# Products queued behind the attention work, four weight-sum tiles, and the first block's attention placed anew

## The chip, the cores and the metric

The kernel runs on one core of a Trainium2 chip. The metric is the device time of one execution in microseconds (us). TensorE (PE) does the matrix products, VectorE (DVE), ScalarE (ACT) and GpSimd (POOL) the elementwise work, and SyncE (SP) issues the transfers. Each engine works through its own instructions in the order in which the program has them.

## The reference

```python
# q, k, v: (8, 8, 576, 64); chunks of 64 tokens, each attends to itself alone
scores = scale * np.matmul(q_c, k_c.transpose(0, 1, 2, 4, 3))
scores = scores - np.max(scores, axis=-1, keepdims=True)
attn = np.exp(scores)
attn = attn / (np.sum(attn, axis=-1, keepdims=True) + 1e-09)
out = np.matmul(attn, v_c)
x = out.transpose(0, 2, 1, 3).reshape(4608, 512)
# layer 1: gated MLP, d_ff 1536
g = x @ w_gate
x = (g * (1.0 / (1.0 + np.exp(-g))) * (x @ w_val)) @ w_out
# layer 2: RMS norm times rms_g, and a gated MLP with weights of its own
xn = x / np.sqrt(np.mean(x * x, axis=-1, keepdims=True) + 1e-06) * rms_g
g = xn @ w_gate2
return (g * (1.0 / (1.0 + np.exp(-g))) * (xn @ w_val2)) @ w_out2
```

## The kernel before

Every matrix product is done as three products of a high part and a low part of its operands (`mm3`). Layer 1 takes the 4608 tokens in nine blocks of 512 and walks for each block through twelve steps f, each of 128 of the 1536 hidden columns (the loop from L1000 on). A step is: `emit_g` (12 matmuls into the bank "g", the sigmoid on ScalarE, the gate product on VectorE), run(0), `emit_v` (12 matmuls into the bank "v", the value product on VectorE, its high part `hh` cast on ScalarE), run(1), `emit_y` of the step before (12 matmuls that add into four output banks), then `lo()`, which is VectorE's low part `hl`, and run(2). The banks "g" and "v" have one buffer each: the matmuls of the next gate can't begin until VectorE has read the gate of this step.

What the three runs of a step do stands in a table `at`: a block has 36 positions, three a step, so position 24 is run(0) of step 8. The table places beside layer 1 of a block

- the attention of the next block, four tiles of 128 tokens, beginning at b = 0, 8, 16 and 24: transposes of queries and keys (`trans_att`, or `trans_tok` for the first tiles), scores and exponential (`att_s`), the division (`att_n`), transposes of the probabilities (`att_td` in two halves of eight small transposes on VectorE, for tiles from 8 on; `att_t` through TensorE before), the product with the values (`att_pv`) and the split of x (`att_lo`, whose tiles are `xh` and `xl`);
- the RMS norm of the block before, with a Newton iteration on VectorE and GpSimd at position 26 (L538 to L547) and the scaling at 28 to 34 (L555);
- in blocks 1 to 6 the weights of layer 2, of which sums and differences are formed: each of seven a group is copied by ScalarE (L175), its rest subtracted by GpSimd, and the pair written to memory by SP. These pairs stand in tiles "ws" of which there are two.

Loads of queries, keys and values for a later group are spread over positions by `spread`. In the first block (`head`) each run also holds a conversion of layer-1 weights, `conv1`: ScalarE's rebase and cast, four VectorE instructions (L115, L118, L121, L139) and a low part that SP writes to memory; and the loop issues what is left of the first groups' loads, the list `later`, 16 a step. Layer 2 follows in another loop (from L750 on) that the change does not reach.

Of the kernel before, what the change touches and what calls it, by code (L numbers as in the profile page):

```python
# [9 lines left out]
F32 = mybir.dt.float32  # L10
F32R = mybir.dt.float32r
# [8 lines left out]
def tile_kernel(  # L20
# [17 lines left out]
    nc = tc.nc  # L38
# [3 lines left out]
    P = 128  # L42
# [24 lines left out]
    cv = open_pool(conv, "cv", 3, "right")  # L67
# [84 lines left out]
    HK = KD * P // 2  # L152
# [18 lines left out]

    def comb_split(nm, fp, k):
        t = comb[nm, fp][k]
        w = cv.tile([P, 2, HK], F32R, tag="ws", bufs=2, name=f"ws{nm}{fp}_{k}")
        nc.scalar.copy(w[:, 0], t)  # L175
        nc.gpsimd.tensor_sub(w[:, 1], t, w[:, 0].bitcast(F32))
        nc.sync.dma_start(out=w2_d["gvo".index(nm), fp, :, k], in_=w.bitcast(F32))
# [14 lines left out]
    EARLY = NW // P + 1  # L192
# [20 lines left out]
    def load_qk(g):  # L213
        tq = ax.tile([P, HP, 10, 32], F32, tag="xq", name=f"xq_{g}")
        tk = ax.tile([P, HP, 10, 32], F32, tag="xk", name=f"xk_{g}")
        gt[g] = [tq, tk]
        dmas = []
        for hp in range(HP):
            for t, src in ((tq, q), (tk, k)):
                for o, m, b, s in segs_of(g):  # L220
                    for z in range(4):
                        hpar, e = divmod(z, 2)
                        dmas.append((
                            t[32 * z:32 * z + 32, hp, 2 * o:2 * (o + m), :],
                            src[b, 2 * hp + hpar, s:s + m * CH, 32 * e:32 * e + 32].rearrange(
                                "(tb p) i -> p tb i", p=32
                            ),
                        ))
        return dmas

    def load_v(g):
        if g == 0:
            tv = xp.tile([P, HP, len(groups[g]), D], F32, tag="xl", name="xv_0")
        else:
            tv = ax.tile([P, HP, 5, D], F32, tag="xv", name=f"xv_{g}")
        gt.setdefault(g, [None, None]).append(tv)
        dmas = []
        for o, m, b, s in segs_of(g):
            for n in range(m):
                for hpar in range(2):  # L240
                    z = hpar ^ ((groups[g][0] + o + n) % 2)
                    dmas.append((
                        tv[64 * z:64 * z + 64, :, o + n, :],
                        v[b, hpar::2, s + n * CH:s + (n + 1) * CH, :].rearrange("h p d -> p h d"),
                    ))
        return dmas
# [39 lines left out]
    def issue(dmas):  # L286
        for o, i in dmas:
            nc.sync.dma_start(out=o, in_=i)  # L288
# [145 lines left out]
    def emit_g(l, j, f):  # L434
        n = blocks[j][1]
        xh, xl = xhl[l, j]
        wh, wl = w_of(l, j, f, "g")
        g = ps.tile([P, 512], F32, tag="g", name=f"g{l}_{j}_{f}")
        for c in range(KD):
            mm3(g[:, :n], wh[:, c], wl[:, c], xh[:, c, :n], xl[:, c, :n], c == 0, c == KD - 1)  # L440
        sg = hp_.tile([P, 512], F32, tag="sg", name=f"sg{l}_{j}_{f}")
        nc.scalar.activation(sg[:, :n], g[:, :n], AF.Sigmoid)  # L442
        nc.vector.tensor_mul(sg[:, :n], g[:, :n], sg[:, :n])  # L443
        return sg

    def emit_v(l, j, f, sg):
        n = blocks[j][1]
        xh, xl = xhl[l, j]
        wh, wl = w_of(l, j, f, "v")
        vv = ps.tile([P, 512], F32, tag="v", name=f"v{l}_{j}_{f}")  # L450
        for c in range(KD):
            mm3(vv[:, :n], wh[:, c], wl[:, c], xh[:, c, :n], xl[:, c, :n], c == 0, c == KD - 1)
        nc.vector.tensor_mul(sg[:, :n], vv[:, :n], sg[:, :n])  # L453
        hh = hp_.tile([P, 512], F32R, tag="hh", name=f"hh{l}_{j}_{f}")
        hl = hp_.tile([P, 512], F32R, tag="hl", name=f"hl{l}_{j}_{f}")
        nc.scalar.copy(hh[:, :n], sg[:, :n])  # L456
        hid[l, j, f] = (hh, hl)
        return lambda: nc.vector.tensor_sub(hl[:, :n], sg[:, :n], hh[:, :n].bitcast(F32))  # L458

    def emit_y(l, j, f):  # L460
        n = blocks[j][1]
# [111 lines left out]
    def spread(l, j, pos, n, make):  # L573
        todo = []

        def step(z):
            if z == 0:
                todo.extend(make())
            issue(todo[z * len(todo) // n:(z + 1) * len(todo) // n])

        for z in range(n):
            put(l, j, pos + z, lambda z=z: step(z))

    for x, (l, j) in enumerate(seq):
        if x + 1 < len(seq):
            nl, nj = seq[x + 1]
            if nl == 0:
                for n, i in enumerate(tiles_of(nj)):
                    b = 8 * n
                    if i >= EARLY:  # L590
                        put(l, j, b - 1, lambda i=i: trans_att(i))
                    else:
                        put(l, j, b, lambda i=i: trans_tok(i, ("a0", "a1")))
                    e = 1 if i < 8 else 0
                    put(l, j, b + 1 + e, lambda i=i: att_s(i))
                    put(l, j, b + 2 + e, lambda i=i: att_n(i))
                    if i < 8:
                        put(l, j, b + 6, lambda i=i: att_t(i))
                    else:
                        put(l, j, b + 3, lambda i=i: att_td(i, 0))  # L600
                        put(l, j, b + 4, lambda i=i: att_td(i, 1))
                    e = 0 if i < 8 else 1
                    put(l, j, b + 8 - e, lambda i=i, nj=nj: att_pv(i, nj))
                    put(l, j, b + 9 - e, lambda i=i, nj=nj: att_lo(i, nj))
                    for c in (2 * i, 2 * i + 1):
                        g = where[c][0]
                        if g > 0 and c == groups[g][-1] and g + 2 < len(groups):
                            spread(l, j, b + 1, 8, lambda g=g: load_qk(g + 2))
                            spread(l, j, b + 9, 3, lambda g=g: load_v(g + 2))
        if x > 0 and seq[x - 1][0] == 0:  # L610
            pj = seq[x - 1][1]
            for d in range(KD):
                put(l, j, 3 + 2 * d, lambda pj=pj, d=d: rms_sq(pj, d))
            put(l, j, 12, lambda pj=pj: rms_split(pj))
            put(l, j, 14, lambda pj=pj: rms_mm(pj))
            for z in range(4):
                put(l, j, 18 + 2 * z, lambda pj=pj, z=z: rms_rec(pj, z))
            put(l, j, 26, lambda pj=pj: rms_newton(pj))
            for d in range(KD):
                put(l, j, 28 + 2 * d, lambda pj=pj, d=d: rms_x(pj, d))  # L620
# [3 lines left out]
    for (nm, f), (j, pos) in zip(w2, slots):  # L624
# [3 lines left out]
        if f >= NP2:  # L628
            fp = f - NP2
# [279 lines left out]
    with tc.manual_schedule():  # L909
# [48 lines left out]
        later = load_v(1) + load_qk(2) + load_v(2)  # L958
# [35 lines left out]
        lp = 0  # L994
# [5 lines left out]
        for n, (l, j, f) in enumerate(iters):  # L1000
            def run(p):
                for fn in at.get(3 * n + p, ()):
                    fn()

            head = (l, j) == (0, 0)
            if (j, f) == (1, 0):
                conv.close()
                cv = open_pool(conv, "cv2", 2, "right")
            if (j, f) == (NB - 1, 0):
                conv.close()  # L1010
                attn.close()
                X2 = open_pool(two, "x2", 1, "right")
                x_load(0, 0)
                xops = x_prep(0, 0)
            if (j, f) == (NB - 1, 8):
                x_load(0, 1)
                xops = xops + x_prep(0, 1)
            if (j, f) == (NB - 1, 8):
                load_ring(16)

            if head:
                issue(later[lp:lp + 16])
                lp += 16
            if n + 2 < len(iters) and n + 2 >= NF:
                load_lo(*iters[n + 2])
            sg = emit_g(l, j, f)
            run(0)
            if head:
                conv1(3 * f + 7)
            lo = emit_v(l, j, f, sg)  # L1030
            run(1)
            if head:
                conv1(3 * f + 8)
            if prev is not None:
                emit_y(*prev)
                if prev[2] == NF - 1:
                    evac_y(*prev[:2])
            lo()
            run(2)
            if head:  # L1040
                conv1(3 * f + 9)
            if j == NB - 1 and f >= 2:
                for _ in range(3 if f > 6 else 2):
                    if xops:
                        xops.pop(0)()
            prev = (l, j, f)
# [108 lines left out]
```

## Time and profile before

| what | value |
|---|---|
| median of 3 runs | 1873.76 us (1873.12 to 1874.0) |
| the profiled execution's own time | 1874.61 us |
| its span in the profile | 1872.8 us |
| mean granted TensorE clock | 0.983 |
| PE busy | 1787.9 us, 95% of the span |
| DVE busy | 1262.1 us, 67% |
| ACT busy | 743.5 us, 40% |
| POOL busy | 385.6 us, 21% |
| moved by DMA | 379.60 MB, mean 203 GB/s |

The busy shares are means over stages that differ much, and the span is what the profiler saw between the first and the last instruction; the execution's own time lies 1.8 us above it. A granted clock of 1 is 2.4 GHz, and 0.5 is 1.2 GHz. In a row of a timeline the brackets hold the engine's idle time just before the instruction and what ended it.

### The profile page before, as it was taken

How to read it: one execution, taken by the hardware profiler on the slowest of the kernel's cores; microseconds unless marked ns; L12 is line 12 of the kernel's file. 1: busy time of each engine (PE TensorE's matmuls, PEld its weight loads, DVE VectorE, ACT ScalarE, POOL GpSimd, SP SyncE). 2: the span in 40 equal slices, each digit the busy share in tenths (PEclk: the TensorE clock that was granted, in tenths of full speed). 3: DMA queues.
4: the chain of work that ended last, by engine and by line, in shares of the span. 5: the costliest groups of instructions: out<-in, count | busy, mean ns of one | idle time of the engine just before them, and what ended most of it. 6: DMA issues, size and time to landing. Idle time of an engine off the chain costs nothing.

```text
span 1872.8 us, 31073 instructions
## 1 busy us (share of the span) xinstructions
PE 1787.9 (95%) x11070; PEld 1520.7 (81%) x11070; DVE 1262.1 (67%) x2366; ACT 743.5 (40%) x1312; POOL 385.6 (21%) x391
## 2 busy tenths in 40 slices
PE   6688999999999999999999999999999999999999
PEld 4466877777787777777888878998898889999999
DVE  7787686776777777776654465864594568468465
ACT  4454343433344342443323233533353345235334
POOL 1000333234342342534011310110020011002000
PEclk7899999999999999999999999999999999999999
DMA  9785657767577766566343567677667767887875
GB/s 245 164 254 161 170 179 218 212 172 213 162 216 196 224 200 207 174 194 208 107 138 94 192 172 250 196 242 208 200 210 227 209 188 221 264 264 252 279 246 180
DMA packets 389546, 379.60 MB, mean 203 GB/s; under 512 B 204560, under 2 KB 240400, under 8 KB 389392
## 3 DMA queue, kind: packets, MB, share of 16 engines
q1 hardware_dynamic: 389392, 377.61, 67.7%
q8 instruction: 89, 1.46, 0.3%
q14 instruction: 65, 0.53, 0.1%
HBM read 316.15 MB, written 61.34 MB: 202 GB/s over the span
## 4 chain that ended last, share of the span: by engine, by line
PE 64%; DVE 13%; DMA 7%; ACT 6%; SPq 4%; issue 3%; POOL 3%; ACTq 0%; DVEq 0%; POOLq 0%
PE ygA L862 5%; PE yvA L862 4%; PE g L430 3%; DVE pT L364 3%; PE g L432 3%; PE g L431 3%; PE v L430 3%; PE v L432 2%; PE v L431 2%; PE ygC L862 2%; PE y L430 2%; PE y L432 2%; PE y L431 2%; SPq L288 2%; PE yvC L862 2%
## 5 line engine op out<-in xcount | busy, mean ns | idle before, releaser
L430 PE MATMUL g<-xh,wg 128*128 128x512 f32 x432 | 176.7, 409 | 27.6 <-DVE sg L443 26.5
L456 ACT CAST hh<-sg 128x512 fp32r<-128x512 f32 x108 | 67.0, 621 | 273.7 <-DVE sg L453 273.7
L431 PE MATMUL g<-xl,wg 128*128 128x512 f32 x432 | 172.5, 399 | 1.6 <-DVE xl L424 1.6
L443 DVE TENSOR_TENSOR sg<-g,sg 128x512 f32<-128x512 f32 x108 | 74.0, 685 | 147.2 <-ACT sg L442 147.0
L432 PE MATMUL g<-xh,lg 128*128 128x512 f32 x432 | 172.0, 398 | 0.7 <-DMA lg<-lo_scratch 0.7
L430 PE MATMUL v<-xh,wv 128*128 128x512 f32 x432 | 171.2, 396 | 1.3 <-DVE sg L453 1.3
L430 PE MATMUL y<-hh,wo 128*128 128x512 f32 x432 | 172.2, 399 | 0.0
L431 PE MATMUL y<-hl,wo 128*128 128x512 f32 x432 | 169.6, 393 | 2.0 <-DVE hl L458 1.9
L431 PE MATMUL v<-xl,wv 128*128 128x512 f32 x432 | 169.0, 391 | 0.0
L432 PE MATMUL v<-xh,lv 128*128 128x512 f32 x432 | 168.9, 391 | 0.0
L432 PE MATMUL y<-hh,lo 128*128 128x512 f32 x432 | 168.7, 390 | 0.0
L802 POOL TENSOR_TENSOR h<-h,h 128x512 f32<-128x512 f32 (+1 forms) x30 | 37.1, 1236 | 551.4 <-DVE h L780 551.4
L364 DVE STREAM_TRANSPOSE pT<-p 32x128 f32<-32x128 f32 x448 | 135.4, 302 | 12.8 <-POOL p L348 6.6
L838 DVE TENSOR_TENSOR hl<-h,hh 128x512 fp32r<-128x512 f32 (+1 forms) x180 | 121.4, 699 | 13.7 <-ACT hh L837 13.6
L430 PEld LDWEIGHTS g<-xh,wg 128*128 128x128 f32 x432 | 83.0, 192 | 54.1 <-DVE sg L443 35.4
L837 ACT CAST hh<-h 128x512 fp32r<-128x512 f32 (+1 forms) x180 | 99.0, 576 | 41.9 <-PE yvA L862 26.6
L763 ACT ACTIVATE sig<-sgt 128x512 f32<-128x512 f32 (+1 forms) x90 | 53.0, 589 | 156.8 <-DVE sgt L771 156.8
L442 ACT ACTIVATE sg<-g 128x512 f32<-128x512 f32 x108 | 64.5, 598 | 93.9 <-PE g L432 93.2
L453 DVE TENSOR_TENSOR sg<-v,sg 128x512 f32<-128x512 f32 x108 | 73.4, 680 | 40.4 <-PE v L432 37.8
L348 POOL TENSOR_TENSOR p<-p,r 128x512 f32<-128x512 f32 x36 | 39.5, 1098 | 292.2 <-DVE r L347 242.7
L764 DVE TENSOR_TENSOR sgt<-sgt,sig 128x512 f32<-128x512 f32 (+1 forms) x90 | 57.7, 641 | 61.6 <-ACT sig L763 61.6
L432 PEld LDWEIGHTS g<-xh,lg 128*128 128x128 f32 x432 | 83.4, 193 | 19.4 <-DMA lg<-lo_scratch 1.1
(770 smaller groups left out, 4686.3 us busy)
## 6 DMA issues: line engine op xcount, KB each, us to landing
wrg<-w_scratch SPq DMA_DIRECT2D x210, 256.0 KB, 3.1
wrv<-w_scratch SPq DMA_DIRECT2D x210, 256.0 KB, 3.1
wro<-w_scratch SPq DMA_DIRECT2D x210, 256.0 KB, 3.0
lg<-lo_scratch SPq DMA_DIRECT2D x96, 256.0 KB, 2.9
lv<-lo_scratch SPq DMA_DIRECT2D x96, 256.0 KB, 3.2
lo<-lo_scratch SPq DMA_DIRECT2D x96, 256.0 KB, 4.0
w_scratch<-wsg SPq DMA_DIRECT2D x42, 256.0 KB, 2.1
w_scratch<-wsv SPq DMA_DIRECT2D x42, 256.0 KB, 2.5
```

Source lines behind the costliest of these rows:

```text
L364: nc.vector.transpose(out=pT[o:o + 32, :, r:r + 32], in_=pt[r:r + 32, :, z, b * 32:b * 32 + 32])
L430: nc.tensor.matmul(o, sh, mh, start=first, stop=False, skip_group_check=free)
L431: nc.tensor.matmul(o, sh, ml, start=False, stop=False, skip_group_check=free)
L432: nc.tensor.matmul(o, sl, mh, start=False, stop=last, skip_group_check=free)
L442: nc.scalar.activation(sg[:, :n], g[:, :n], AF.Sigmoid)
L443: nc.vector.tensor_mul(sg[:, :n], g[:, :n], sg[:, :n])
L453: nc.vector.tensor_mul(sg[:, :n], vv[:, :n], sg[:, :n])
L456: nc.scalar.copy(hh[:, :n], sg[:, :n])
L764: nc.vector.tensor_mul(t[:, :tw], src[:, :tw], sg[:, :tw])
L837: nc.scalar.copy(hh[:, :tw], src)
L838: nc.vector.tensor_sub(hl[:, :tw], src, hh[:, :tw].bitcast(F32))
L862: mm = lambda l, r, first, last: nc.tensor.matmul(oo, l, r, start=first, stop=last, skip_group_check=True)
```

## The change

It has five parts. The tiles "ws" become four. `emit_g` and `emit_v` no longer queue their products; they return them, and the loop queues the gate product after run(0) and the value product, with the cast to `hh`, after run(1). In the first block the four tiles begin at 0, 11, 19 and 26. The loads that follow tile 4 begin nine positions later. The list `later` is issued 32 a step.

```diff
     def comb_split(nm, fp, k):
         t = comb[nm, fp][k]
-        w = cv.tile([P, 2, HK], F32R, tag="ws", bufs=2, name=f"ws{nm}{fp}_{k}")
+        w = cv.tile([P, 2, HK], F32R, tag="ws", bufs=4, name=f"ws{nm}{fp}_{k}")
...
         nc.scalar.activation(sg[:, :n], g[:, :n], AF.Sigmoid)
-        nc.vector.tensor_mul(sg[:, :n], g[:, :n], sg[:, :n])
-        return sg
+        return sg, lambda: nc.vector.tensor_mul(sg[:, :n], g[:, :n], sg[:, :n])
...
-        nc.vector.tensor_mul(sg[:, :n], vv[:, :n], sg[:, :n])
         hh = hp_.tile([P, 512], F32R, tag="hh", name=f"hh{l}_{j}_{f}")
         hl = hp_.tile([P, 512], F32R, tag="hl", name=f"hl{l}_{j}_{f}")
-        nc.scalar.copy(hh[:, :n], sg[:, :n])
         hid[l, j, f] = (hh, hl)
-        return lambda: nc.vector.tensor_sub(hl[:, :n], sg[:, :n], hh[:, :n].bitcast(F32))
+
+        def product():
+            nc.vector.tensor_mul(sg[:, :n], vv[:, :n], sg[:, :n])
+            nc.scalar.copy(hh[:, :n], sg[:, :n])
+
+        return product, lambda: nc.vector.tensor_sub(hl[:, :n], sg[:, :n], hh[:, :n].bitcast(F32))
...
-                    b = 8 * n
+                    b = 8 * n if x else (0, 11, 19, 26)[n]
...
-                            spread(l, j, b + 1, 8, lambda g=g: load_qk(g + 2))
-                            spread(l, j, b + 9, 3, lambda g=g: load_v(g + 2))
+                            d = 10 if i < EARLY else 1
+                            spread(l, j, b + d, 8, lambda g=g: load_qk(g + 2))
+                            spread(l, j, b + d + 8, 3, lambda g=g: load_v(g + 2))
...
             if head:
-                issue(later[lp:lp + 16])
-                lp += 16
+                issue(later[lp:lp + 32])
+                lp += 32
...
-            sg = emit_g(l, j, f)
+            sg, product = emit_g(l, j, f)
             run(0)
+            product()
             if head:
                 conv1(3 * f + 7)
-            lo = emit_v(l, j, f, sg)
+            product, lo = emit_v(l, j, f, sg)
             run(1)
+            product()
```

On VectorE, in block 2 from the end of step 8 to step 9, the order before is this (in a name such as `sg_2_9` stand block and step; `p` and `pT` are a tile's probabilities, `ms` and `rr` the RMS norm's):

```order
L458 TENSOR_TENSOR hl_2_8_3907<-sg_2_8_3880,hh_2_8_3906 128x512
L343 TENSOR_REDUCE r_3959<-p_3928 128x8
L346 TENSOR_SCALAR r_3959<-r_3959 128x8
L347 RECIPROCAL r_3959<-r_3959 128x8
L544 SCALAR_TENSOR_TENSOR ms_3544<-ms_3544,rr_3546 128x512
L547 SCALAR_TENSOR_TENSOR rr_3546<-ms_3544,rr_3546 128x512
L443 TENSOR_TENSOR sg_2_9_3996<-g_2_9_3983,sg_2_9_3996 128x512
L364 STREAM_TRANSPOSE pT_3999<-p_3928 32x4x32 x8
L453 TENSOR_TENSOR sg_2_9_3996<-v_2_9_4020,sg_2_9_3996 128x512
L364 STREAM_TRANSPOSE pT_3999<-p_3928 32x4x32 x8
L555 SCALAR_TENSOR_TENSOR ysb_0_1_3130<-ysb_0_1_3130,rg,rr_3546 128x512
```

And now:

```order
L460 TENSOR_TENSOR hl_2_8_3906<-sg_2_8_3880,hh_2_8_3905 128x512
L343 TENSOR_REDUCE r_3959<-p_3926 128x8
L346 TENSOR_SCALAR r_3959<-r_3959 128x8
L347 RECIPROCAL r_3959<-r_3959 128x8
L546 SCALAR_TENSOR_TENSOR ms_3544<-ms_3544,rr_3546 128x512
L549 SCALAR_TENSOR_TENSOR rr_3546<-ms_3544,rr_3546 128x512
L364 STREAM_TRANSPOSE pT_3998<-p_3926 32x4x32 x8
L443 TENSOR_TENSOR sg_2_9_3996<-g_2_9_3983,sg_2_9_3996 128x512
L364 STREAM_TRANSPOSE pT_3998<-p_3926 32x4x32 x8
L557 SCALAR_TENSOR_TENSOR ysb_0_1_3130<-ysb_0_1_3130,rg,rr_3546 128x512
L457 TENSOR_TENSOR sg_2_9_3996<-v_2_9_4020,sg_2_9_3996 128x512
```

The gate product has moved behind the first eight transposes, and the value product behind the second eight and a scaling.

On ScalarE, in step 8 of the same block, the order before (`wsv` are weight sums):

```order
L442 ACTIVATE sg_2_8_3880<-g_2_8_3867 128x512
L456 CAST hh_2_8_3906<-sg_2_8_3880 128x512
L336 ACT_TABLE_LOAD
L336 ACTIVATE p_3928<-p_3928 128x512
L175 CAST wsv_3_3940<-wtv_3_3886 128x256
```

And now:

```order
L442 ACTIVATE sg_2_8_3880<-g_2_8_3867 128x512
L336 ACT_TABLE_LOAD
L336 ACTIVATE p_3926<-p_3926 128x512
L175 CAST wsv_3_3938<-wtv_3_3885 128x256
L458 CAST hh_2_8_3905<-sg_2_8_3880 128x512
```

The cast to `hh` has moved behind a table load, the exponential of the tile and a weight sum's copy.

On SP, in the first block's steps 1 to 3, the order before (`xq_609` and `xk_610` are queries and keys of the next group, `xq_154` and `xk_155` those of the group that is due; `w64g`, `w64v`, `w64o` are weights):

```order
L288 DMA xq_609<-in_q_dram 32x6x32 x4
L96 DMA w64g_0_625<-in_moe_w_gate_dram 128x4x256
L943 DMA lo_scratch<-lo_0_1_530 128x512
L288 DMA xk_610<-in_k_dram 32x6x32 x4
L96 DMA w64v_0_668<-in_moe_w_val_dram 128x4x256
L943 DMA lo_scratch<-lg_0_2_589 128x512
L288 DMA xk_155<-in_k_dram 32x10x32 x4
L288 DMA xq_154<-in_q_dram 32x10x32 x4
```

And now:

```order
L288 DMA xq_154<-in_q_dram 32x10x32 x4
L946 DMA lo_scratch<-lv_0_1_517 128x512
L96 DMA w64g_0_635<-in_moe_w_gate_dram 128x4x256
L946 DMA lo_scratch<-lo_0_1_530 128x512
L96 DMA w64v_0_674<-in_moe_w_val_dram 128x4x256
L946 DMA lo_scratch<-lg_0_2_605 128x512
L288 DMA xk_155<-in_k_dram 32x10x32 x4
L288 DMA xv_156<-in_v_dram 64x4x64 x10
L96 DMA w64o_0_722<-in_moe_w_out_dram 128x1024
```

The next group's loads have left this stretch; the due group's queries stand together ahead of it, and its last four keys and its values behind the weights of step 2.

## Rows read from the trace of the kernel before

**Rows 1.** Busy time by stretch of the span (columns as in the first line).

```profile
core 0: us, PE busy (x) PEld busy (x) DVE busy (x) ACT busy (x) POOL busy (x), PEclk, DMA share, GB/s
0.00:45.00 45.00, 26.89 (x329) 20.57 (x330) 32.42 (x68) 20.88 (x38) 4.88 (x10) 0.73 1.01 250
45.00:175.00 130.00, 99.68 (x602) 78.02 (x601) 105.89 (x190) 63.01 (x102) 4.19 (x4) 0.89 0.71 191
175.00:950.00 775.00, 747.26 (x4811) 596.87 (x4810) 566.75 (x1208) 304.49 (x511) 262.57 (x289) 0.99 0.64 188
950.00:1873.00 923.00, 914.03 (x5332) 825.24 (x5330) 557.02 (x902) 355.17 (x663) 113.94 (x88) 1.00 0.69 214
```

**Rows 2.** Waits of PE, 175 to 950: us in total, times, longest.

```profile
PE g L430 <- DVE sg L443: 21.8, 18, 2.8
PE s L315 <- DVE xl L424: 3.5, 8, 0.7
```

**Rows 3.** Timeline of PE, block 2, step 3: start, length, instruction, idle before.

```profile
322.44 0.69 PE L430 MATMUL g<-xh,wg 128*128 128x512 f32 x1 [2.00 <-DVE sg L443]
```

**Rows 4.** Timeline of ACT, block 2, steps 2 and 3.

```profile
313.95 0.41 ACT L175 CAST wso<-cro 128x256 fp32r<-128x256 f32 x1 [5.99 <-DMA w_scratch<-wso]
...
321.07 0.59 ACT L442 ACTIVATE sg<-g 128x512 f32<-128x512 f32 x1
```

**Rows 5.** Waits of ACT on the weight sums' stores, 175 to 950.

```profile
ACT wsv L175 <- DMA w_scratch<-wsv: 42.4, 25, 5.1
ACT wso L175 <- DMA w_scratch<-wso: 40.7, 25, 6.0
ACT wsg L175 <- DMA w_scratch<-wsg: 30.5, 21, 3.9
```

**Rows 6.** Busy time after the stall at 322.44, and in block 7.

```profile
320.00:326.00 6.00, 4.00 (x11) 2.81 (x11) 4.20 (x9) 2.07 (x5) 5.76 (x6) 0.72 0.50 175
...
858.00:900.00 42.00, 41.98 (x269) 33.63 (x268) 27.15 (x63) 16.80 (x29) 18.48 (x20) 1.00 0.64 196
```

**Rows 7.** Waits of DVE, 45 to 175.

```profile
DVE sg L443 <- ACT sg L442: 13.5, 10, 2.6
DVE kT L299 <- DMA xk<-in_k_dram: 8.5, 1, 8.5
```

**Rows 8.** Timeline of DVE, block 2, steps 8 and 9.

```profile
385.77 1.22 DVE L544 SCALAR_TENSOR_TENSOR ms<-ms,rr 128x512 f32<-128x512 f32 x1 [2.71 <-POOL ms L543]
...
388.05 0.68 DVE L443 TENSOR_TENSOR sg<-g,sg 128x512 f32<-128x512 f32 x1
388.65 2.50 DVE L364 STREAM_TRANSPOSE pT<-p 32x128 f32<-32x128 f32 x8
...
394.47 1.06 DVE L555 SCALAR_TENSOR_TENSOR ysb<-ysb,rg,rr 128x512 f32<-128x512 f32 x1
```

**Rows 9.** Timeline of PE, block 2, first matmul of gate step 10.

```profile
389.36 0.39 PE L430 MATMUL g<-xh,wg 128*128 128x512 f32 x1
```

**Rows 10.** Timeline of ACT, block 2, step 8.

```profile
379.12 0.62 ACT L456 CAST hh<-sg 128x512 fp32r<-128x512 f32 x1 [4.17 <-DVE sg L453]
379.75 1.28 ACT L336 ACT_TABLE_LOAD   x1
381.05 0.63 ACT L336 ACTIVATE p<-p 128x512 f32<-128x512 f32 x1
```

**Rows 11.** Timeline of DVE, first block.

```profile
70.18 0.42 DVE L115 TENSOR_SCALAR cmv<-w64v 128x512 uint32<-128x512 uint32 x1
...
72.57 0.68 DVE L453 TENSOR_TENSOR sg<-v,sg 128x512 f32<-128x512 f32 x1
...
82.39 0.71 DVE L299 STREAM_TRANSPOSE kT<-xk 128x512 f32<-128x512 f32 x1 [8.52 <-DMA xk<-in_k_dram]
```

**Rows 12.** Timeline of SP's queue, first block.

```profile
62.77 1.97 SPq L288 DMA_DIRECT2D xk<-in_k_dram  x4
...
68.81 0.38 SPq L96 DMA_DIRECT2D w64o<-in_moe_w_out_dram  x1
```

**Rows 13.** Timeline of ACT, first block.

```profile
73.51 0.66 ACT L107 ACTIVATE cro<-w64o 128x512 f32<-128x512 f32 x1 [3.49 <-DMA w64o<-in_moe_w_out_dram]
```

## Prediction, made before the changed kernel ran

> **What bounds the kernel now.** I read the busy table of four stretches first, then the waits of the engine that sets the pace in each, then single stalls in the timeline. The table [rows 1] cuts the span of 1872.8 us into loading and first attention (0 to 45), the first block (45 to 175), eight blocks that are almost alike (175 to 950) and layer 2. In layer 2 TensorE is idle for 9 of 923 us, and the diff does not touch it; the first 45 us run code that the change leaves alone. So two stretches count. From 45 to 175 VectorE is the fuller engine, 105.9 busy of 130 against TensorE's 99.7. From 175 to 950 TensorE sets the time: 747.3 of 775, so 27.7 us idle.
>
> The steady blocks first. TensorE's waits there [rows 2] are 21.8 us in 18 stalls of the gate matmuls on VectorE's gate product and 3.5 us of the score matmuls on a low half; the other 2.4 of the 27.7 lie in waits of under 1 us. One such stall, in block 2, is the row at 322.44 [rows 3]: the first matmul of a gate bank had to wait 2.00 us until VectorE had read the bank. VectorE was not slow there: its product waited for the sigmoid, and ScalarE stood at a copy of a weight sum, 5.99 us behind the DMA that still read its buffer, so that the next sigmoid came only at 321.07 [rows 4]. In this stretch such copies wait 42.4, 40.7 and 30.5 us [rows 5], 113.6 in all; only what falls ahead of a sigmoid reaches TensorE. A stall of this size costs twice: from 320 to 326 the mean granted clock is 0.72 [rows 6], between the two levels of 1.2 and 2.4 GHz, which is 6 x 0.28 = 1.7 us of work. Three of the 18 stalls were over 2 us; I put 3 x 1.7 = 5 us to them.
>
> In the first block VectorE waits 13.5 us for sigmoids (10 times) and once 8.5 us for a key load [rows 7]; these 22.0 are nearly all of its idle 24.1.
>
> **Four weight-sum tiles.** A copy now waits for the DMA of the fourth buffer before it, not the second. In a group of seven copies the first four find free buffers. The waits of up to 6 us ahead of sigmoids go, the small stalls with them, since they follow from the same late chain; block 7, which has no weight sums, runs 41.98 of 42 us on TensorE now [rows 6]. I take off all of 27.7 + 5 = 32.7 us.
>
> **Products behind the attention work.** No instruction is added. On ScalarE the cast of the value product moves with it. In most runs this costs nothing: a gate bank is wanted again two thirds of a step later, and VectorE has room, as block 7 shows. Where a tile's chain runs into the RMS work it has none. In block 2 before the change, VectorE waits 2.71 us for GpSimd (385.77), then takes two steps of the Newton iteration, the gate product at 388.05, the first half of the tile's transposes (2.50 us) and the value product [rows 8]; TensorE came for the bank at 389.36 [rows 9], 0.63 us after the product's end at 388.73. Afterwards:
> - The cast (379.12 before) stands behind a table load of 1.28, the exponential at 381.05 [rows 10] and a weight-sum copy; the low half waits for the cast, and the row sums stand behind the low half. By these lengths about 0.35 us more for the chain.
> - The first transposes stand ahead of the gate product: 2.50 more. So the product comes 2.85 later, less the 0.63 of room: 2.2. The stalls that are removed let TensorE arrive 2.6 earlier, and VectorE's chain, which starts from a matmul, only about 1.9 (an estimate from its small idle time here); that adds 0.7. Stall at gate step 10: 2.9.
> - The value product stands behind the second transposes (2.5) and a scaling of 1.06 more, some 4 us later than now, of which 2.9 has been paid; about 1.5 at value step 10.
>
> That is 4.4 in each of blocks 1 to 6, 26; block 7, without copies, 2.7. What waits behind: the two products hold up hl and the next sigmoid's product, so I add 0.5 in six blocks for the score matmuls behind a late xl (3.0), 0.9 three times for step 1, where VectorE also waits for a stored tile (2.7), and 0.5 a block for the clock, a third of the 1.7 above (3.5). Sum 38. No row of before shows a product behind the transposes, so the bounds are wide. Below: if VectorE has caught up when it comes there, 13 (under 2 a block). Above: a half of the transposes costs 2.5 at most, nearly all of it, 2.0, on each of 28 tiles: 56. I take 38, since it is worked out from rows of that very place. Steady blocks: -32.7 + 38 = +5.
>
> **First block: tiles and loads placed anew.** The work of a step on VectorE stays: three conversions of 2.4 us (70.18 to the product at 72.57 [rows 11]), two products, a low half, about 11 us, with TensorE below it. So what matters is VectorE's waits.
> - The 8.52 us wait at 82.39 [rows 11] is a transpose of tile 5's keys. SP had issued this group's loads mixed with those of the next group (four in 1.97 us, [rows 12]). The next group now starts nine positions later, 32 a step are issued instead of 16, and the transposes stand at position 10. All are issued by about 60; the wait goes.
> - The sigmoid waits become, step by step: 1.0 (the division of tile 4 now fills the rest), 0.64, 0, 0.58, 2.0, 0, 0, 2.0, 0.58, that is 6.8, and the 2.5 of the last step stays. Where work of a run now precedes the product it fills the sigmoid's latency; where a table load comes between, the 2.0 stays.
> - New: an output weight (issued at 68.81 [rows 12], used by ScalarE at 73.51 after 3.49 of waiting [rows 13]) is now wanted at about 72.1, since VectorE is no longer held; 1.8 of wait. And tile 7's scores come right behind the low half of tile 6: 1.0.
>
> Waits 22.0 before, 6.8 + 2.5 + 1.8 + 1.0 = 12.1 after: -10. Tile 7's division (1.8) leaves the path, 0.7 is lost where block 1 starts nearer to it, and I add one for the clock, which the gap had lowered: -12. Bounds: -15 if the two new waits stay away, +2 if every load moved forward costs more than it frees.
>
> Here a rule bears on it. The rows show SP needing about half a microsecond for each of these loads [rows 12] while the 16 engines are busy at 0.71 in this block and at 1.01 in the first 45 us [rows 1]. The Trainium skill, "DMA: Bandwidth & Descriptors", section "Issuing engines are not separate DMA queues", says that DMAs end up on the same 16 engines and interleave whoever starts them, and that issue time is usually small relative to the transfer. By the rows the queue of issues is the limit and reordering it is a gain; by the rule, loads brought forward take their share from the weight loads beside them, and the gain would shrink from 12 us to the third rival's 5.
>
> **Sum.** 1874.6 (the profiled run's own time) - 12 + 5 = 1867.9. The median of the runs shown is 0.85 below the profiled run, so 1867. The forecast's own range is 1859 to 1875.
>
> **Rivals.**
> 1. The added tiles pay in full and VectorE absorbs the new order. For it: VectorE is 566.8 of 775 busy [rows 1], a quarter free, and the waits that go leave it ahead. Against: room of 0.63 us beside 2.5 us of transposes. Added 13 instead of 38: 1874.6 - 12 - 32.7 + 13 = 1842.9, so 1842.
> 2. Slower. Transposes ahead of a product hold both banks at every tile, not only at the fourth of a block. Place: steps in which a half of 2.50 us stands in run 0 or run 1; price 2.0 each, 28 tiles, 56 us: 1874.6 - 12 - 32.7 + 56 = 1885.9, so 1885. It decides from an added 12 + 32.7 = 45 on, 1.6 a tile. For it: a bank has one buffer, so each late product is TensorE's loss. Against: three tiles of four have no RMS chain beside them, and now have slack.
> 3. The loads brought forward delay the weight loads of the first block. For it: the shares 0.71 and 1.01 and the 3.49 us that ScalarE already waits for a weight [rows 13]. Against: the total of bytes is the same, and the next group moves back. Price: 28 loads come earlier, at 0.5 us each 14 us of SP's queue [rows 12] ahead of weight loads, and half of that, 7, would show as waits of the conversions. 12 becomes 5: 1874.6 - 5 + 5 - 0.85 = 1874.
>
> **How the numbers follow.** Forecast 50 in 100, rival 1 20, rival 2 18, rival 3 12. What a measurement of this kernel can tell from no change is about 0.2%, that is 1870.0 to 1877.5. Forecast: 34 faster, 12 within, 4 slower; rival 1: 20 faster; rival 2: 1 within, 17 slower; rival 3: 1, 10 and 1. Together: faster 0.55, within 0.23, slower 0.22. The range goes from rival 1's 1842 to just under rival 2's, 1884; about half of each of these two lies outside.
>
> **What would show it.** First block: VectorE's wait on a key load gone, its sigmoid waits near 9 us; if waits of ScalarE on weight loads grow by over 5 us, rival 3. Steady blocks: ScalarE's waits on the weight-sum DMAs near zero, else the added tiles don't do what they say; TensorE's stalls on the gate product no longer in steps 3 and 7 but in step 10, each near 2.9, with value stalls behind them. No stalls there is rival 1; stalls at tiles in other steps as well is rival 2. The forecast falls if TensorE's idle time from 175 to 950 comes out below 15 or above 45 us.

## The result, and the profile after

The changed kernel takes 1858.9 us (1857.6 to 1861.5, 4 runs) against 1873.9 before on the same chip: a ratio of 0.9918, 95% interval 0.9901 to 0.9935. It is faster by 15 us, a difference clear of no change; the forecast was 1867, its own range 1859 to 1875, the whole range 1842 to 1884. The profiled execution has a span of 1857.4 us, 15.4 less than before.

To see where these 15 us went I cut both spans at the first sigmoid of a block, ScalarE's `sg<-g` (times in us):

| stretch | before | after | forecast of the difference |
|---|---|---|---|
| to block 0's first sigmoid | 44.6 | 45.0 | 0 |
| first block | 144.0 | 142.5 | -12 |
| blocks 1 to 7 | 779.5 | 765.6 | +5 |
| from block 8's first sigmoid on | 904.7 | 904.3 | 0 |

So the total came out near the forecast with its two halves exchanged: the first block gave almost nothing, the steady blocks gave nearly all. In single profiles kernels with the same first block differ by up to 2 us there, so its 1.5 is not told from none. The busy table of the changed kernel by the same stretches as [rows 1], which also has its columns:

```profile
0.00:45.00 45.00, 25.95 (x327) 19.72 (x328) 32.38 (x68) 20.38 (x38) 4.87 (x10) 0.77 0.99 245
45.00:175.00 130.00, 102.91 (x607) 79.99 (x606) 105.73 (x192) 63.70 (x102) 4.43 (x4) 0.91 0.72 201
175.00:950.00 775.00, 755.56 (x4903) 606.58 (x4902) 585.39 (x1224) 302.56 (x517) 259.89 (x289) 1.00 0.66 191
```

TensorE's idle time from 175 to 950 is 19.4 us instead of 27.7. What TensorE waits for there, to be laid beside [rows 2]:

```profile
PE g L430 <- DVE sg L443: 13.7, 8, 2.0
PE v L430 <- DVE sg L457: 4.6, 5, 0.9
PE s L315 <- DVE xl L424: 1.1, 3, 0.4
```

Eight gate stalls are left of 18, and value stalls are new. Seven of the eight are the first matmul of gate step 10, one in each of blocks 1 to 7. ScalarE's waits for the weight sums' stores, 113.6 us in [rows 5], are now 23.8:

```profile
ACT wso L175 <- DMA w_scratch<-wso: 12.8, 12, 2.4
...
ACT wsv L175 <- DMA w_scratch<-wsv: 10.4, 6, 1.8
...
ACT wsg L175 <- DMA w_scratch<-wsg: 0.6, 2, 0.5
```

The place that the forecast named, block 2's steps 8 and 9, on VectorE (compare [rows 8]; start, length, instruction, idle before):

```profile
379.25 1.21 DVE L546 SCALAR_TENSOR_TENSOR ms<-ms,rr 128x512 f32<-128x512 f32 x1 [2.41 <-POOL ms L545]
...
381.52 2.51 DVE L364 STREAM_TRANSPOSE pT<-p 32x128 f32<-32x128 f32 x8
384.06 0.69 DVE L443 TENSOR_TENSOR sg<-g,sg 128x512 f32<-128x512 f32 x1
384.78 2.53 DVE L364 STREAM_TRANSPOSE pT<-p 32x128 f32<-32x128 f32 x8
387.34 0.75 DVE L557 SCALAR_TENSOR_TENSOR ysb<-ysb,rg,rr 128x512 f32<-128x512 f32 x1
388.01 0.68 DVE L457 TENSOR_TENSOR sg<-v,sg 128x512 f32<-128x512 f32 x1
```

and on TensorE, where [rows 9] had no wait:

```profile
382.49 0.39 PE L432 MATMUL y<-hh,lo 128*128 128x512 f32 x1
384.81 0.68 PE L430 MATMUL g<-xh,wg 128*128 128x512 f32 x1 [1.93 <-DVE sg L443]
```

TensorE is ready at 382.88; the gate product waits its turn behind 2.51 us of transposes until 384.06.

In the first block VectorE's waits, which were one key load and the sigmoids [rows 7], have become:

```profile
DVE sg L443 <- ACT sg L442: 11.4, 8, 2.0
DVE cmo L115 <- DMA w64o<-in_moe_w_out_dram: 4.8, 1, 4.8
DVE cmg L115 <- DMA w64g<-in_moe_w_gate_dram: 2.0, 1, 2.0
DVE sg L457 <- PE v L432: 1.4, 1, 1.4
DVE m L329 <- PE s L315: 1.0, 1, 1.0
DVE hl L460 <- ACT hh L458: 0.7, 1, 0.7
```

The key load's 8.5 us are gone, and 6.8 us on two weights have come. SP's queue says why:

```profile
61.50 0.39 SPq L96 DMA_DIRECT2D w64g<-in_moe_w_gate_dram  x1
...
67.13 8.05 SPq L288 DMA_DIRECT2D xv<-in_v_dram  x10
75.29 0.54 SPq L96 DMA_DIRECT2D w64o<-in_moe_w_out_dram  x1
```

The output weight that was issued at 68.81 [rows 12] is issued at 75.29, behind the ten value loads that 32 a step brought forward. The gate weight, which VectorE waits 2.0 us for, had been issued at 53.40 and is issued at 61.50, behind queries and keys. ScalarE starts on the output weight at 79.93, at 73.51 before [rows 13]:

```profile
79.93 0.68 ACT L107 ACTIVATE cro<-w64o 128x512 f32<-128x512 f32 x1 [8.14 <-DMA w64o<-in_moe_w_out_dram]
```

From issue to landing this weight takes the same time in the kernel before (first line) and in the changed one (second), so all of its delay lies ahead of its issue:

```profile
DMA to landing us min/median/max: 4.6/4.6/4.6
...
DMA to landing us min/median/max: 4.5/4.5/4.5
```

### The profile page after: what moved, and what is told of

Read it like the earlier page. It is cut to its first block, busy times and chain, and to the rows that moved or that the text cites. A ratio compares the mean times of both kernels' runs of the same rounds, so it can differ in the third digit from the quotient of the medians.

```text
span 1857.4 us, 31012 instructions
## 1 busy us (share of the span) xinstructions
PE 1783.3 (96%) x11070; PEld 1519.3 (82%) x11070; DVE 1271.5 (68%) x2366; ACT 738.0 (40%) x1312; POOL 382.7 (21%) x391
## 4 chain that ended last, share of the span: by engine, by line
PE 78%; DVE 11%; DMA 4%; ACT 2%; issue 2%; SPq 2%; POOL 1%; DVEq 0%; ACTq 0%; POOLq 0%
PE ygA L865 4%; PE v L430 4%; PE v L432 4%; PE v L431 4%; PE g L430 4%; PE y L430 4%; PE g L432 4%; PE g L431 4%; PE yvA L865 4%; PE y L432 4%; PE y L431 4%; PE ygC L865 2%; DVE pT L364 2%; PE yvC L865 2%; PE ygD L865 1%
## 5 line engine op out<-in xcount | busy, mean ns | idle before, releaser
L460 DVE TENSOR_TENSOR hl<-sg,hh 128x512 fp32r<-128x512 f32 x108 | 85.0, 787 | 72.7 <-ACT hh L458 72.7
L430 PEld LDWEIGHTS v<-xh,wv 128*128 128x128 f32 x432 | 81.3, 188 | 29.3 <-DVE sg L457 11.8
```

Of the source, the lines that this page charges most:

```text
L430: nc.tensor.matmul(o, sh, mh, start=first, stop=False, skip_group_check=free)
L460: return product, lambda: nc.vector.tensor_sub(hl[:, :n], sg[:, :n], hh[:, :n].bitcast(F32))
```

## The experiments

Three rounds of four kernels, each round on one chip beside the kernel before; numbers of different rounds are compared by their ratios to it. The kernel before took 1873.5 us in the first and third round and 1870.9 in the second, so a time of the second round reads some 3 us low against a range that was set from the first. Edits are shown against the kernel before or against the changed kernel, whichever is nearer.

### The parts one by one

Four weight-sum tiles alone:

```diff
-        w = cv.tile([P, 2, HK], F32R, tag="ws", bufs=2, ...)
+        w = cv.tile([P, 2, HK], F32R, tag="ws", bufs=4, ...)
```

> The kernel before with four weight-sum tiles and nothing else. Theory T (the tiles give the whole gain of the steady blocks, and the new order takes part of it back): the sum of the prediction took off 27.7 us of stalls and 5 of clock; I expect nearly that, 28 below before, so 1841 to 1852. Rival Q (the order is what frees the sigmoids, since VectorE no longer stands at a product while attention work waits): the tiles alone give under 4 us, 1870 to 1875, and TensorE's gate stalls in steps 3 and 7 stay.

Measured: 1841.1 us, ratio 0.9829 (0.9812 to 0.9846). That is T's, at the lower end of its range, and this one number gives twice what the whole change gives. TensorE's waits from 175 to 950 in this kernel, all of them:

```profile
PE s L315 <- DVE xl L424: 2.7, 3, 0.9
PE xb L405 <- DVE ms L527: 0.4, 1, 0.4
PE y L431 <- DVE hl L458: 0.2, 1, 0.2
```

No gate stall is left. In its block 2, the RMS step on VectorE and TensorE's first matmul of gate step 10:

```profile
377.50 1.21 DVE L544 SCALAR_TENSOR_TENSOR ms<-ms,rr 128x512 f32<-128x512 f32 x1 [2.72 <-POOL ms L543]
...
381.62 0.39 PE L430 MATMUL g<-xh,wg 128*128 128x512 f32 x1
```

The products queued later, alone (two tiles, first block as before):

```diff
-        nc.vector.tensor_mul(sg[:, :n], g[:, :n], sg[:, :n])
+        return sg, lambda: nc.vector.tensor_mul(sg[:, :n], g[:, :n], sg[:, :n])
...
             run(0)
+            product()
```

> The kernel before with only the products queued behind run(0) and run(1). T: ScalarE's waits on the weight-sum stores stay, and stalls at gate step 10 and value step 10 (1.9 and 0.9 in the changed kernel, seven blocks) are added: 5 to 20 us above before, 1879 to 1894. Q: 1857 to 1862, the whole gain.

Measured: 1894.8 us, ratio 1.0116 (1.0100 to 1.0132): slower by 21 us, a microsecond beyond T's range. The gate stalls grow:

```profile
PE g L430 <- DVE sg L443: 31.8, 18, 2.7
PE s L315 <- DVE xl L424: 2.1, 2, 1.2
PE v L430 <- DVE sg L457: 1.1, 1, 1.1
PE y L431 <- DVE hl L460: 0.7, 2, 0.4
```

The first block's placement and loads, alone:

```diff
-                    b = 8 * n
+                    b = 8 * n if x else (0, 11, 19, 26)[n]
...
-                issue(later[lp:lp + 16])
+                issue(later[lp:lp + 32])
```

> The kernel before with only the first block's tile positions, the later loads of the group after, and 32 loads a step. In the changed kernel the first block ends only 1.1 us earlier. T: the ten value loads, 8.05 us of SP's queue ahead of an output weight, take back what the key load frees, whatever the order of the products: 1871 to 1876. Rival H (the placement is worth its 8 us, and the new order of the products takes them back in the first block): 1864 to 1868.

Measured: 1871.0 us, ratio 0.9984 (0.9973 to 0.9995). It lies at the lower edge of T's range, some 3 us under the kernel before. In the profile VectorE waits 5.6 us on the output weight and no longer on the key load, as T says; the first block itself takes 145.4 us, no less than the 144.0 of the kernel before and the 145.4 of the tiles alone, so the 3 us are not found there.

Tiles and order, without the first block's part:

> The changed kernel with the first block's placement and loads as before. T: the steady blocks keep their gain of 14, the first block is as before or 1 us longer: 1858 to 1864. H: the new order without the new placement loses in the first block what the placement gives, 1865 to 1872.

Measured: 1860.4 us, ratio 0.9928 (0.9913 to 0.9943), in T's range. Laid over one another the ratios give the whole: tiles -32 us, order on top of them +18.5, placement on top of both -1.9. The first two are clear of the intervals, of some 3 us to either side; the third is not told from none.

### What the first block loses, and what the order costs

The list `later` issued 16, 20, 5 and 5 in the first four steps:

```diff
-                issue(later[lp:lp + 32])
-                lp += 32
+                nl_ = (16, 20, 5, 5)[f] if f < 4 else 0
+                issue(later[lp:lp + nl_])
+                lp += nl_
```

> The changed kernel with the list later issued 16, 20, 5 and 5 in the first four steps, in place of 32 and the rest. Theory L (the ten value loads, 8.05 us of SP's queue ahead of an output weight, are what took the first block's gain back): VectorE's waits of 4.84 and 2.03 us on weights go and the key wait does not return, 4 to 6 us less, 1853 to 1856. Rival P (the first block is held by its last steps, where tile 7 now stands, and a gain ahead of them is lost there): under 2 us, 1857 to 1860.

Measured: 1849.8 us, ratio 0.9892 (0.9873 to 0.9912) against the changed kernel's 0.9918: 5 us less by the ratio, as L expects. The intervals touch, but the first block says the same: 134.7 us in the profile against 142.5, and 134.2 to 136.1 in the three kernels that have this first block against 140.4 to 142.5 in the three that have the changed kernel's. In it the weight is issued ahead of the values:

```profile
66.53 0.39 SPq L96 DMA_DIRECT2D w64o<-in_moe_w_out_dram  x1
...
70.34 4.40 SPq L288 DMA_DIRECT2D xv<-in_v_dram  x5
```

Neither weight wait is among VectorE's waits of the block any more, and the key wait has not returned. The queue's order was the cause of the two waits.

Step 9's two products ahead of the runs again, in blocks 1 to 7:

```diff
+            early = j > 0 and f == 9
+            if early:
+                product()
             run(0)
-            product()
+            if not early:
+                product()
```

(and the same around run(1)).

> The changed kernel with both products of step 9 queued ahead of run(0) and run(1) again, in blocks 1 to 7 alone. Theory T (the order costs what the transposes of the fourth tile put ahead of the two products of step 9): the stalls of 1.93 and 0.93 us go in seven blocks, with a little of the clock, 18 to 20 us, 1838 to 1842, where the kernel with the tiles alone is. Rival N (the Newton chain holds VectorE up whatever stands behind it, the wait moves to the low half or the scaling): under 8 us, 1851 to 1859.

Measured: 1848.7 us, ratio 0.9885 (0.9864 to 0.9906): 6 us less than the changed kernel. By time that lies between the theories, by the ratio inside N's "under 8 us"; but N's mechanism is not what is seen. In blocks 1 and 4 to 6 the stalls of 1.93 and 0.93 are gone and a block takes 107.2 or 107.3 us instead of 109.4 to 109.8. But blocks 2 and 3 take 112.9 and 109.6: there something else comes through. ScalarE early in block 2:

```profile
310.85 0.41 ACT L175 CAST wso<-cro 128x256 fp32r<-128x256 f32 x1 [6.60 <-DMA w_scratch<-wso]
...
312.39 0.60 ACT L458 CAST hh<-sg 128x512 fp32r<-128x512 f32 x1
```

VectorE's product, which this cast reads, is done at 310.87:

```profile
310.18 0.69 DVE L457 TENSOR_TENSOR sg<-v,sg 128x512 f32<-128x512 f32 x1
```

The cast to `hh`, queued after run(1), stands behind the weight sums' copies of that run, which the 6.60 us held up, and starts 1.5 us late; VectorE's low half waits 2.16 us for it. Whether this is all that blocks 2 and 3 lose isn't shown: ScalarE's waits on loads of the output weight, which stand near the ends of blocks, grew as well, to 27.0 us in the stretch from 12.0 in the changed kernel.

Four tiles, placement and split loads, with the products where they were before:

> The kernel before with four weight-sum tiles (1841.1 alone), the first block's placement, and its loads issued 16, 20, 5 and 5; products in the old order. L: the placement, worth 2.5 us alone, gains the 4 to 6 of the weight waits, 1833 to 1836. P: 1838 to 1841.

Measured: 1834.6 us, ratio 0.9811 (0.9790 to 0.9832) against 0.9829 for the tiles alone: 3 us, intervals overlapping. The time itself is in L's range, the ratio between L and P; it is not told from no gain. The first block takes 137.9 us in its profile against 145.4.

The same with the new order in the first block alone (the edit against the changed kernel, and likewise around run(1)):

```diff
+            late = head
+            if not late:
+                product()
             run(0)
-            product()
+            if late:
+                product()
```

> As the run before, and the new order of the products in the first block alone. The first block is 141.8 us with the new order against 145.4 without, both with four tiles and the old placement. If that is the order's and adds to the placement: 3 us less than the run before, 1830 to 1833. If it was the key load's arrival (waits of 11.9 and 10.0 us) and not the order: the same as the run before within 1.5 us.

Measured: 1832.7 us, ratio 0.9799 (0.9779 to 0.9818), 2 us less than the run before, between the two expectations and inside the intervals; the first block is 136.1, and 134.7 and 134.2 in the two other kernels with that first block, against 137.9 once without the order. Whether the order gains anything in the first block stays open.

### Which product costs, and what the waits of the copies cost

The kernel with step 9's products first, and five tiles:

> The changed kernel with step 9's products first (1848.7 with four weight-sum tiles) and five tiles. With four, blocks 2 and 3 took 112.9 and 109.6 us in the profile and the others 107.3; there a copy of a weight sum waited 6.60 us for its store, with the cast to hh behind it. Theory W (the new order lets the cast stand behind those waits, and one more tile shortens them): blocks 2 and 3 come to 107 to 109, 1840 to 1845. Rival (the stores are late on SP's queue whatever the tiles, or the wait is another): 1846 to 1850.

Measured: 1846.7 us, ratio 0.9852 (0.9833 to 0.9871). By the ratio that is 6 us under the kernel with four, in W's direction, with intervals that overlap; the time itself is in the rival's range. Blocks 2 and 3 took 109.9 and 109.0 in the profile, still over 107.3. The copies' waits for the stores fell from 24.7 to 10.4 us, a wait of 5.2 among them, and those on the output weight stayed, 25.2. So the copies' waits may be part of it; it isn't decided.

The best kernel with five tiles:

> The best kernel so far (four tiles, placement, loads split, new order in the first block alone; 1832.7) with five tiles. In its steady blocks TensorE waits under 4 us in all, so both theories expect the same within 2 us, 1830 to 1834; more than that would say that the tiles still bound it.

Measured: 1832.4 us, ratio 0.9780 (0.9759 to 0.9800), by time the same as with four, as expected, and by the ratio 3.5 us less with intervals that overlap. Both beat the kernel before by 2%, the changed one by more than 1%.

Four tiles and the gate product alone moved, then the value product alone, both without the first block's part (the edit of the first against the changed kernel):

```diff
             product, lo = emit_v(l, j, f, sg)
+            product()
             run(1)
-            product()
```

> Four tiles and only the gate product queued behind run(0); the value product and its cast stand where they stood. Tiles alone took 1841.1, tiles with both products moved 1860.4. Theory G (the gate product behind the first transposes is what costs, 1.93 of the 2.86 us in each block): 1853 to 1857. Rival V (the value product with the cast to hh, which holds up the low half and the row sums behind it, costs most): 1842 to 1848.

> Four tiles and only the value product and its cast queued behind run(1); the gate product stands where it stood. G: 0.93 us in each block and little else, 1845 to 1850. V: 1853 to 1860.

Measured: gate alone 1843.8 us, ratio 0.9840 (0.9822 to 0.9859), not told from the tiles alone; value alone 1876.2 us, ratio 1.0011 (0.9997 to 1.0026), which eats the tiles' whole gain. G falls, and V holds beyond its range: moving one product costs nearly twice what moving both costs. TensorE's waits from 175 to 950 with the gate product alone,

```profile
PE g L430 <- DVE sg L443: 8.2, 7, 1.2
PE s L315 <- DVE xl L424: 1.5, 4, 0.4
```

and with the value product alone:

```profile
PE v L430 <- DVE sg L457: 20.0, 14, 2.9
PE xb L405 <- DVE ms L529: 1.6, 1, 1.6
PE s L315 <- DVE xl L424: 1.3, 6, 0.3
```

VectorE in block 1 of the latter:

```profile
277.97 0.68 DVE L443 TENSOR_TENSOR sg<-g,sg 128x512 f32<-128x512 f32 x1
278.57 5.04 DVE L364 STREAM_TRANSPOSE pT<-p 32x128 f32<-32x128 f32 x16
283.65 0.75 DVE L557 SCALAR_TENSOR_TENSOR ysb<-ysb,rg,rr 128x512 f32<-128x512 f32 x1
284.31 0.68 DVE L457 TENSOR_TENSOR sg<-v,sg 128x512 f32<-128x512 f32 x1
```

Both halves of the transposes and a scaling stand ahead of the value product, and TensorE waits 2.94 us at value step 10, and 2.89 to 3.05 in the other six blocks. With both products moved it waits 1.93 at the gate and, in blocks 3 to 7, 0.93 at the value, 2.86: the same lateness, paid in two parts. With the gate alone, the value product and its cast keep their place, VectorE's chain starts 0.7 us earlier against TensorE, and 1.23 is all. So by value step 10 the two stalls of the changed kernel are one delay, which the place of the value product makes; its cast moves with it and was not tried apart. The gate product's place alone costs its 1.23 a block, 6 us over blocks 1 to 7 in the profile (the row below, against that of the tiles alone), which a first block of 142.1 us against 145.4 half hides in the total:

```profile
186.70:937.30 750.60, 740.90 (x4832) 596.82 (x4831) 584.53 (x1217) 300.75 (x512) 263.69 (x289) 1.00 0.67 195
```

Why is one stall of 2.94 dearer than two of the same sum? In part it is the granted clock. Six us from the stall at value step 10 of block 1, value product alone:

```profile
285.05:291.05 6.00, 6.00 (x48) 4.42 (x49) 4.81 (x7) 2.17 (x6) 0.93 (x1) 0.72 0.71 211
```

A mean of 0.72 lies between 1.2 and 2.4 GHz, 6 x 0.28 = 1.7 us of work. It follows the stall of step 10 in five of the seven blocks; in the changed kernel in two of seven. The sum over blocks 1 to 7 is kept by the busy time of the same matmuls (x4831 or x4832), each kernel from its own first sigmoid of block 1 to that of block 8: the tiles alone,

```profile
190.00:934.40 744.40, 740.69 (x4831) 597.78 (x4830) 575.81 (x1217) 299.99 (x512) 263.34 (x289) 1.00 0.67 197
```

the changed kernel,

```profile
187.50:953.10 765.60, 746.16 (x4832) 598.99 (x4830) 581.43 (x1217) 300.21 (x512) 259.89 (x289) 1.00 0.66 192
```

the value product alone,

```profile
191.00:971.00 780.00, 753.56 (x4832) 602.88 (x4831) 576.67 (x1217) 298.83 (x513) 258.65 (x289) 0.99 0.65 189
```

and, for the kernel before,

```profile
188.60:968.10 779.50, 751.76 (x4831) 600.60 (x4830) 571.35 (x1217) 305.18 (x512) 262.57 (x289) 0.99 0.64 188
```

Over the tiles alone, the value product costs 22.7 us of idle time and 12.9 of slower matmuls; the changed kernel 15.7 and 5.5; the kernel before 24.0 and 11.1. So half of what the value product costs beyond both products together is slower matmuls (7.4 us), and half is idle time (7.0): the second stall is missing in two blocks of the changed kernel, and the value product alone has small waits elsewhere.

## Why the prediction was right, and where its steps were not

- **Tiles.** 27.7 + 5 = 32.7 us were taken off. The tiles alone took off 32 by the ratio, and every gate stall went. The five us put to the clock were too few by the rows above (11.1 of slower matmuls), but 3.3 us of small stalls remained and the profiles differ by some us elsewhere. Right.
- **Products behind the attention work.** The sign, the place and the cause were right: the fourth tile's transposes, at gate and value step 10 of blocks 1 to 7. The size was not: 38 forecast, 18.5 measured on top of the tiles by the ratios, 21.2 in the profiles of blocks 1 to 7. The step that failed is "That is 4.4 in each of blocks 1 to 6": it is 2.86 (1.93 and 0.93) where it is seen in full. At the gate step the 2.50 us of transposes less the 0.63 of room, 1.9, are what came; the 0.35 for a later chain and the 0.7 for a TensorE that arrives earlier came to nothing together. For with the tiles alone TensorE does not arrive earlier, measured from VectorE's chain, but later. It comes to the bank 4.1 us after VectorE's RMS step begins (381.62 and 377.50 in block 2), and 3.6 after it in the kernel before (389.36 [rows 9] and 385.77 [rows 8]); with the value product moved it is 3.6 again (382.88 and 379.25 in the changed kernel). At the value step 0.93 came for 1.5, where the scaling takes 0.75 us and 1.06 was counted. Of the 3.0 us added for the scores the changed trace has 1.1; of the 2.7 for step 1 it has no wait of TensorE, only one of 0.9 us of VectorE on a stored tile; the clock, put at 3.5, took 5.5.
- **First block.** 12 forecast, 1.5 in the profile, 1.9 to 3 by the ratios; the 1.5 is not clear of the spread between profiles. The key load's wait went as worked out, though the last keys were issued by 66.7 and not by 60. The step that failed is "an output weight (issued at 68.81 [rows 12] ...) is now wanted at about 72.1": I kept the time of issue from the old trace, although the new order has ten value loads ahead of it, and took 0.5 us a load where those ten take 0.8. The weight came 6.4 us later, and VectorE waited 4.8 for it and 2.0 for one more weight, 6.8 where 1.8 was forecast. VectorE's waits from 45 to 175 add up to 21.3 us instead of the 12.1 forecast: 5.0 of the difference are the weights, 2.1 the sigmoids (11.4 for 9.3), the rest small waits. With the loads split the block takes 134.7: most of the forecast's gain was there to be had.
- **The rivals.** The third's mechanism, loads ahead of weights, is what happened, and the 7 us that it named are near what the split gave back, 7.8 in the profile and 5 by the ratio. The sign that the forecast set for it was not met: ScalarE's waits on weight loads grew from 11.0 to 14.8 us, by less than 5. It isn't the engines' bandwidth that the rows show for the output weight but its place in the issuing queue: SP's ten issues last 8.05 us, the weight lands 4.5 us after its own issue as before, and moving the ten, with the same bytes, takes the wait away. The Trainium skill ("DMA: Bandwidth & Descriptors", section "Issuing engines are not separate DMA queues") says that issue time is usually small relative to the transfer. For each load by itself the trace agrees, 0.6 to 1.0 us of issue and 2.4 to 3.8 to landing; but one queue's issues follow one another, and ten of them add up. The first rival named no stalls at step 10, and they are there; its 13 us for the order is nevertheless nearer to the measured 18.5 than the forecast's 38. The second, transposes at every tile, is out: the stalls stand at the fourth tile.

Two errors of opposite sign, 10 us less gained in the first block and 19 us less lost in the steady blocks, left 8 us between forecast and result. So the mechanism was right in the steady blocks, and that the total came so near, just under the forecast's own range, is luck.

## What to carry to other kernels

A change of several parts can hide one that costs behind one that gains: here a single number, two tiles to four, is worth 32 us, and the reordering beside it gives back 18.5. When work is queued ahead of a product that another engine waits for, follow the longest block of it (16 transposes, 5.0 us) to the bank it holds, and count one delay once. When loads are brought forward, list what stands behind them in the issuing queue and move its time of issue too.

## What the runs showed of the hardware

The granted clock did not answer stalls of the same length alike: after 1.91 to 1.97 us at gate step 10 the changed kernel ran six us at a mean of 0.72 in blocks 1 and 2 and at 1.00 in blocks 3 to 7. Block 3 and then block 2, with the same number of instructions on VectorE, ScalarE and GpSimd:

```profile
494.39:500.39 6.00, 5.07 (x21) 3.89 (x22) 5.18 (x12) 1.42 (x3) 0.94 (x1) 1.00 0.42 157
384.81:390.81 6.00, 6.00 (x19) 4.80 (x20) 5.18 (x12) 1.43 (x3) 0.94 (x1) 0.72 0.81 241
```

What tells them apart wasn't tried. In block 3 the matmuls ran at speed and the second stall of 0.93 followed (busy 5.07 of 6); in blocks 1 and 2 the slower matmuls filled that time, so part of the clock's loss costs nothing there.
